# Hash attention and a max-out FFN on one core: a head's four bit tests in one, two pair hashes put together, one group hash a unit earlier

## The chip, the cores and the metric

The kernel runs on one core of a Trainium2 chip. The core has five engines that run on their own and meet through semaphores: TensorE (PE), VectorE (DVE), ScalarE (ACT), GpSimd (POOL) and SyncE (SP). The metric is the device time of one execution in microseconds. Before the change it is 268.99 us, the median of three runs (268.82 to 269.55).

## The reference, cut to what matters

```python
q_bits = (np.einsum('bhsd,dk->bhsk', q, proj) > 0)        # proj: 64 x 6
k_bits = (np.einsum('bhsd,dk->bhsk', k, proj) > 0)
mask = q_bucket[:, :, :, None] == k_bucket[:, :, None, :]  # all six bits alike
scores = np.where(mask, scale * np.matmul(q, k.T), -1e9)
attn = softmax(scores)
x = matmul(attn, v)                                        # 4 batches, 8 heads, 768 x 64
h = np.maximum(np.maximum(x @ w1, x @ w2), x @ w3)         # 3072 tokens, 512 -> 768
out = h @ w_out                                            # 768 -> 512
```

## The kernel before, in words

**How the mask is computed.** Each token gets six extra rows beside its 64 features, one for each bit, with the value +0.5 or -0.5. The product of a key's column and a query's column, 70 rows each, then holds the score and a term that is largest where all six bits agree. An exp with a bias makes everything else vanish. So scores of a head can be computed when its tile `S` has both: the features (`pair_place`, `first_place` for the first head, `place` for later ones) and the bits.

**Where the bits come from.** Batch 0 has its eight heads in four pairs (pair 0 is heads 0 and 1). A pair is loaded by `load_pair`, each head and side (side 1 is k, side 0 is q) is turned by three transposes on PE (`pair_turn`, L122), copied from PSUM to a tile `T32` by DVE or ACT (`pair_keep`, L129 or L131), and placed in `S` by POOL (`pair_place`, L136). A hash multiplies `T32` by the projection and tests the sign. There are two ways to do it. By head (`head_hash`, L169, and `head_bits`, L174): four small matmuls and four tests, each of which reads PSUM and writes six rows straight into `S`; a head has four parts, side by half of the tokens (`par`). By pair (`pair_hash`, L149 to L159): one bank for the pair, one test of 128 rows into a tile `bits` (L152), and four transfers on SP's queue (L158) that carry the bits to their rows in `S`. Pairs 0 and 1 go by head, pairs 2 and 3 by pair. Heads of the batches behind come in groups of four (`load_quad`, `turn` L200, `narrow` L205, `place` L210, `quad_hash` L219, whose four transfers at L230 are issued one unit after the hash). Groups are numbered 2 to 7; 2 and 3 are batch 1.

**What sets the order of the work.** The order is written out by hand: the instructions of an engine run in the order of the program. The main loop goes over units: a unit is 128x768 scores of one head (three matmuls of 256 columns in batch 0, two of 384 later, L296) and one exp on ACT (L304). Batch 0 has 48 units, the others 144. Two PSUM buffers hold scores, so the scores of unit n+2 wait for the exp of unit n. In iteration u the program writes the scores of unit u+1, then what `when(u, ...)` has put down for u, then one group of the FFN where there is one, then the bursts put down for u in `todo` (sums of the exps, L351, and their products with v, L373), and at last the hash of a group that `hash_at` names for u. Units 0 to 5 are head 0, 6 to 11 head 1, 12 to 23 heads 2 and 3; heads 4 to 7 begin at unit 24, two units a head for chunk 0 of queries. Units 48 to 59 are batch 1's heads 0 to 3, and from unit 60 on heads 4 to 7, group 3.

**Queues around the change.** Transfers are issued by SP (keys and queries of batch 0, placements of later groups, bits, results), by ACT (queries of pair 0) and by POOL (v, weights, queries and keys of later groups), each in the order of the program. Transfers of SP and ACT share eight completion semaphores in rotation, so an issue waits until the issue eight before it has landed.

**Before the loop.** The loads go out; 11 matmuls on a zero tile (L498) keep PE busy until the first keys are there; then head 0 is turned, hashed and tested part by part, and units 0 and 1 are written. The hash of groups uses another arrangement of the projection, `pj`, which POOL fills (L534 to L536).

Of the kernel before, what the change touches and what calls it, by code (L numbers as in the profile page):

```python
# [11 lines left out]
BF16 = mybir.dt.bfloat16  # L12
AluOp = mybir.AluOpType
# [4 lines left out]
def kernel(  # L18
# [12 lines left out]
    nc = tc.nc  # L31
# [62 lines left out]
    def give(i):  # L94
        free_banks.append(i)
# [70 lines left out]
    def head_hash(bp, pi, side, hd, pars=(0, 1)):  # L166
        for par in pars:
            j = 2 * side + par
            nc.tensor.matmul(bp[Q * j : Q * j + NBITS, 0:HALF], pj2[:, par : 2 * NBITS : 2],  # L169
                             t32[pi][:, side, hd * HALF : (hd + 1) * HALF], start=True, stop=True)  # L170

    def head_bits(bp, pi, side, hd, par):
        j = 2 * side + par
        nc.vector.tensor_scalar(out=s_tile(pi)[D : D + NBITS, 2 * side + hd, par * HALF : (par + 1) * HALF],  # L174
                                in0=bp[Q * j : Q * j + NBITS, 0:HALF], scalar1=0.0, scalar2=0.5,
                                op0=AluOp.is_gt, op1=AluOp.subtract)

    def head_rest(pi, hd):
        i, bp = bank()
        for side in (1, 0):  # L180
            head_hash(bp, pi, side, hd)
        for side, par in ((1, 0), (0, 0), (1, 1), (0, 1)):
            head_bits(bp, pi, side, hd, par)
        give(i)


    def load_quad(side, g, xs, eng):
# [284 lines left out]
    def when(u, f, *args):  # L472
        at.setdefault(u, []).append(lambda: f(*args))

    with tc.manual_schedule():
        load_pair(0, nc.sync, (1,), 0, 1)
        load_pair(0, nc.scalar, (0,), 0, 1)
        nc.sync.dma_start(pst[:], proj.rearrange("(u d) k -> d u k", d=Q))
        nc.vector.memset(warm[:], 0.0)
        make_identity(nc, iden[:])  # L480
        load_pair(0, nc.sync, (1,), 1, 2)
        load_pair(0, nc.scalar, (0,), 1, 2)
        load_pair(1, nc.sync)
        load_pair(2, nc.sync)
        load_pair(3, nc.sync)
        load_quad(1, 2, range(4), nc.sync)
        nc.vector.memset(pj2[:], 0.0)
        nc.vector.memset(ones[:], 1.0)
        for t in at_tiles:
            nc.vector.memset(blocks(t, THIRD)[:, :, THIRD : THIRD + 2], 1.0)  # L490
        for hd in range(2):
            for u in range(2):
                (nc.vector, nc.gpsimd)[hd].tensor_copy(
                    pj2[hd * D + u * Q : hd * D + (u + 1) * Q, hd : hd + 2 * NBITS - 1 : 2], pst[:, u, :])
        load_v(0)
        iw, wp = bank()
        for n in range(11):
            nc.tensor.matmul(wp[:, 0:HALF], warm[:, 0:P], warm[:], start=True, stop=True)  # L498
        give(iw)

        ik, mk = bank()
        iq, mq = bank()
        ib, bk = bank()
        jb, bq = bank()
        pair_turn(0, 1, 0, mk)
        pair_keep(0, 1, 0, mk)
        for par in range(2):
            pair_place(0, 1, par, 0, 1)
        pair_turn(0, 0, 0, mq)
        pair_keep(0, 0, 0, mq, nc.scalar)  # L510
        head_hash(bk, 0, 1, 0, (0,))
        head_bits(bk, 0, 1, 0, 0)
        first_place(0, 0, 0, mq)
        pair_place(0, 0, 1, 0, 1)
        head_hash(bq, 0, 0, 0, (0,))
        head_bits(bq, 0, 0, 0, 0)
        head_hash(mk, 0, 1, 0, (1,))
        head_bits(mk, 0, 1, 0, 1)
        give(ik)
        head_hash(mq, 0, 0, 0, (1,))  # L520
        head_bits(mq, 0, 0, 0, 1)
        give(iq)
        scores(0)
        scores(1)
        pair_turn(0, 1, 1, bk)
        pair_turn(0, 0, 1, bq)
        pair_keep(0, 1, 1, bk)
        give(ib)
        pair_keep(0, 0, 1, bq)
        give(jb)  # L530
        for side in (1, 0):
            for par in range(2):
                pair_place(0, side, par, 1, 2)
        nc.gpsimd.memset(pj[:], 0.0)  # L534
        for x in range(4):
            nc.gpsimd.tensor_copy(pj[x * Q : (x + 1) * Q, :, x : x + 4 * NBITS - 3 : 4], pst[:])  # L536

        for pi, us in ((1, ((0, 1, 0), (0, 0, 0), (3, 1, 1), (4, 0, 1))), (2, ((6, 1, 0), (7, 1, 1), (9, 0, 0), (10, 0, 1))),
                       (3, ((11, 1, 0), (13, 1, 1), (14, 0, 0), (15, 0, 1)))):
            for u, side, hd in us:  # L540
                when(u, pair_group, pi, side, hd, nc.scalar if pi == 1 and hd == 1 else None)
                if pi == 1:
                    for par in range(2):
                        when(u, pair_place, pi, side, par, hd, hd + 1)
                elif hd == 1:
                    for par in range(2):
                        when(u, pair_place, pi, side, par)
        when(2, head_rest, 0, 1)
        when(2, t32.pop, 0)
        when(5, head_rest, 1, 0)  # L550
        when(8, head_rest, 1, 1)
        when(9, t32.pop, 1)
        when(12, pair_hash, 2)
        when(13, t32.pop, 2)
        when(18, pair_hash, 3)
        when(19, t32.pop, 3)
        when(17, load_v, 1)
        for n, u in ((0, 3), (1, 12), (2, 21), (3, 31)):
            when(u, load_weights, n)
        when(13, load_quad, 0, 2, range(4), nc.gpsimd)  # L560
        for u, side, g in ((23, 1, 3), (27, 0, 3)):
            when(u, load_quad, side, g, range(4), nc.sync)
        hash_at = {}
        for g in range(2, NQUAD):
            b2, i2 = divmod(g, 2)
            need = UPB * b2 + 12 * i2
            for n, side in enumerate((1, 0)):
                name = (side, g)
                if g > 3:
                    us = [SPREAD[b2][0] + SPREAD[b2][1] * (8 * i2 + 4 * n + n2) // 4 for n2 in range(4)]  # L570
                    for x in range(4):
                        when(us[0] - 14 + x, load_quad, side, g, (x,), nc.gpsimd)
                else:
                    us = [need - {2: 26, 3: 23}[g] + 4 * n + n2 for n2 in range(4)]
                for n2, u2 in enumerate(us):
                    when(u2, turn, name, n2 // 2, n2 % 2)
                    if n2 % 2:
                        when(u2 + 1, narrow, name, n2 // 2)
                when(us[3] + 3, place, name, range(4))
            hash_at[{2: 32, 3: 48, 4: need - 12}.get(g, need - 9)] = g  # L580
            when({2: 36, 3: 46}.get(g, need - 22), load_v, g)

        ffn, credit = [], 0
        todo = {}
        last_of = {}
        for c, i in sorted(done_at, key=lambda e: done_at[e]):
            d = done_at[c, i] + LAG[c > 2]
            sums, values = burst(c, i)
            pieces = [lambda f=sums: f(0, NM), lambda f=values: f(0, 0, NM), lambda f=values: f(1, 0, NM)]
            for n, f in enumerate(pieces):  # L590
                u = {(0, 0): (16, 17, 20), (1, 0): (21, 22, 24), (2, 0): (26, 27, 29)}.get((c, i), (d, d, d))[n]
                todo.setdefault(u, []).append(f)
            last_of[c] = max(u, last_of.get(c, 0))
        ffn_at = {}
        for c in range(NCH - 1):
            ffn_at.setdefault(last_of[c] + 2, []).append(c)

        for u, (c, h, n) in enumerate(units):
            if c >= 3 and n:
                when(min(u + 2, NU - 1), add, c, h, n)  # L600

        for u in range(NU):
            if 0 < u < NU - 1:
                scores(u + 1)
            for f in at.pop(u, []):
                f()
            for c in ffn_at.get(u, []):
                ffn += ffn_groups(c)
            credit += 1 if u < UPB else 1.15
            if not ffn:  # L610
                credit = 0
            while ffn and credit >= 1:
                credit -= 1
                ffn.pop(0)()
            for f in todo.pop(u, []):
                f()
            if u in hash_at:
                when(u + 1, quad_hash(hash_at[u]))

        for f in ffn[:3]:  # L620
            f()
        ffn = ffn[3:]
        for u in sorted(todo):
            for f in todo[u]:
                f()
        ffn += ffn_groups(NCH - 1)
        for f in ffn:
            f()
# [30 lines left out]
```

## Time and profile before

| | us |
|---|---|
| median of the runs | 268.99 |
| the profiled execution's own time | 268.58 |
| its span, from the first to the last instruction | 266.6 |
| PE busy | 257.9 (97%) |
| DVE busy | 208.9 (78%) |
| ACT busy | 177.3 (67%) |
| POOL busy | 69.9 (26%) |

In the rows of the profile, `MATMUL sc<-S` are scores, `ACTIVATE AT<-sc` are exps, `ms` is one of four PSUM banks, `T` is `T32` or `T16`, and `pj` stands for both arrangements of the projection. A row of the timeline has the start in us, the length, engine, line, operation, what it writes and reads, the shape and how many instructions were merged into it; in brackets stands the idle time of the engine before it and what ended that. SP's landings have no rows of their own: they are seen in what waits for them.

### The profile page before, as it was taken

Reading aid. Unit: us, or ns where it says so; the run is one execution under the profiler, and the core shown is the slowest. Engines: PE = TensorE matmul, PEld = TensorE weight load, DVE = VectorE, ACT = ScalarE, POOL = GpSimd, SP = SyncE. Lnnn points to the kernel's source line nnn. Section 1 sums busy time; section 2 is a strip of 40 time slices with the busy share of each in tenths; the row PEclk is TensorE's granted clock in tenths of the full one; section 3 lists DMA queues with packets and bytes.
Section 4 is the critical chain, followed back from the end, with each engine's and each line's share of the span. In section 5 each row is a group of like instructions: output and inputs, shape, how many; then the busy total and the mean of one; then the engine's idle time right before and its main releaser. Section 6 shows DMA issues by size and latency. Waiting matters only on the chain.

```text
span 266.6 us, 6482 instructions
## 1 busy us (share of the span) xinstructions
PE 257.9 (97%) x2505; PEld 154.4 (58%) x2505; DVE 208.9 (78%) x493; ACT 177.3 (67%) x257; POOL 69.9 (26%) x132
## 2 busy tenths in 40 slices
PE   7899999999799999999999999999999999999995
PEld 4555557885566575555555554555555555554552
DVE  2897685987499999978998997899849785888361
ACT  3596785676758694984869578484895859581322
POOL 3588652355032535240141612011000000000000
PEclk9999999999999999999999999999999999999999
DMA  6977999969703791982054472802030003000303
GB/s 203 316 156 135 230 234 212 245 114 233 185 22 86 159 231 18 234 222 53 4 167 131 56 182 43 204 8 61 15 118 4 0 2 119 2 0 2 118 0 118
DMA packets 20717, 30.95 MB, mean 116 GB/s; under 512 B 2608, under 2 KB 15248, under 8 KB 20688
## 3 DMA queue, kind: packets, MB, share of 16 engines
q0 software_dynamic: 8128, 13.37, 26.6%
q1 hardware_dynamic: 12128, 16.66, 21.8%
q10 hardware_dynamic: 432, 0.52, 0.6%
q8 instruction: 19, 0.31, 0.5%
q14 instruction: 10, 0.08, 0.1%
HBM read 25.17 MB, written 6.29 MB: 118 GB/s over the span
## 4 chain that ended last, share of the span: by engine, by line
PE 84%; DVE 7%; ACT 5%; issue 3%; DVEq 0%; ACTq 0%
PE ms L406 31%; PE sc L296 21%; PE ms L373 11%; PE ms L450 10%; ACT AT L304 4%; PE ms L351 3%; PE ms L219 3%; DVE ht L415 2%; DVE ad L327 1%; PE ms L498 1%; PE ms L122 1%; PE ms L149 1%; DVE T L131 1%; PE ms L169 1%; DVE S L174 1%
## 5 line engine op out<-in xcount | busy, mean ns | idle before, releaser
L304 ACT ACTIVATE AT<-sc 128x768 f16<-128x768 f32 x192 | 152.3, 816 | 62.2 <-PE sc L296 60.7
L406 PE MATMUL ms<-xT,w_sb 128*128 128x384 f16 (+1 forms) x648 | 114.8, 307 | 0.1
L296 PE MATMUL sc<-S 72*128 72x384 bf16 (+1 forms) x432 | 93.6, 308 | 3.3 <-ACT AT L304 1.8
L406 PEld LDWEIGHTS <-w_sb 128*128 128x128 f16 x648 | 62.7, 97 | 35.9 <-issue 0.4
L415 DVE TENSOR_TENSOR ht<-ht,ms 128x384 f16<-128x384 f16 (+1 forms) x108 | 54.3, 504 | 24.4 <-PE ms L406 13.4
L296 PEld LDWEIGHTS <-S 72*128 72x128 bf16 (+1 forms) x432 | 39.4, 98 | 35.7 <-issue 15.5
L205 POOL TENSOR_SCALAR T<-T 128x768 bf16<-128x768 f32 x24 | 22.8, 952 | 95.4 <-issue 50.5
L450 PE MATMUL ms<-wout_sb,ht 128*128 128x512 f16 x138 | 35.5, 378 | 0.0
L373 PE MATMUL ms<-AT,vo 128*32 128x385 f16 (+3 forms) x864 | 35.2, 309 | 0.3 <-DVE ht L415 0.3
L327 DVE TENSOR_TENSOR ad<-ad,AT 128x768 f16<-128x768 f16 x48 | 26.6, 553 | 2.1 <-ACT AT L304 1.3
L373 PEld LDWEIGHTS <-vo 128*32 128x32 f16 x864 | 22.6, 96 | 9.6 <-issue 1.8
L200 DVE STREAM_TRANSPOSE T<-nat 128x384 f32<-128x384 f32 x48 | 27.0, 565 | 0.2 <-DMA nat<-in_q_dram 0.2
L327 DVE TENSOR_TENSOR ad<-AT,AT 128x768 f16<-128x768 f16 x48 | 26.2, 546 | 0.2 <-ACT AT L304 0.2
L411 ACT CAST ht<-ms 128x384 f16<-128x384 f32 x36 | 17.3, 479 | 8.1 <-PE ms L406 8.1
L380 DVE SCALAR_TENSOR_TENSOR xT<-ms,sv,rb 128x384 f16<-128x384 f32 (+1 forms) x36 | 19.8, 567 | 1.4
L450 PEld LDWEIGHTS <-ht 128*128 128x128 f16 x138 | 13.3, 97 | 13.0 <-issue 0.3
L454 ACT COPY osb<-ms 128x512 f32<-128x512 f32 x21 | 12.2, 585 | 8.2 <-PE ms L450 6.3
L330 DVE TENSOR_TENSOR ad<-ad 128x384 f16<-128x384 f16 x32 | 15.5, 484 | 1.1
L136 POOL TENSOR_SCALAR S<-T 64x384 bf16<-64x384 f32 (+1 forms) x23 | 14.2, 617 | 5.0 <-DVE T L131 3.5
L358 DVE STREAM_TRANSPOSE ys<-ms 128x384 f32<-128x384 f32 (+1 forms) x18 | 9.6, 532 | 6.2 <-PE ms L351 6.2
L194 POOL DMA_DIRECT2D nat<-in_q_dram x20 | 11.1, 560 | 0.1
L413 DVE CAST ht<-ms 128x256 f16<-128x256 f32 x18 | 7.4, 413 | 4.0 <-PE ms L406 3.9
(48 smaller groups left out, 123.0 us busy)
## 6 DMA issues: line engine op xcount, KB each, us to landing
out_dram<-osb SPq DMA_DIRECT2D x21, 256.0 KB
S<-T SPq DMA_DIRECT2D x48, 96.0 KB
nat<-in_q_dram POOLq DMA_DIRECT2D x20, 192.0 KB, 6.7
vo<-in_v_dram POOLq DMA_DIRECT2D x8, 384.0 KB, 6.2
nat<-in_k_dram POOLq DMA_DIRECT2D x16, 192.0 KB, 5.7
w_sb<-in_moe_w_dram POOLq DMA_DIRECT2D x3, 768.0 KB, 6.9
nat<-in_k_dram SPq DMA_DIRECT2D x10, 192.0 KB
nat<-in_k_dram SPq DMA_DIRECT2D x3, 384.0 KB
```

The costliest lines, as they stand in the source:

```text
L200: nc.vector.transpose(t32[name][:, u, half * HALF : (half + 1) * HALF], i_)
L205: nc.gpsimd.tensor_scalar(out=t16[name][:, u, :], in0=t32[name][:, u, :], scalar1=RS, scalar2=1.0, op0=AluOp.mult, op1=AluOp.mult)
L296: nc.tensor.matmul(views[j], s_of[kn][0 : D + bits, kx, m * P : (m + 1) * P], s_of[qn][0 : D + bits, qx, q0 : q0 + w], start=True, stop=True)
L304: nc.scalar.activation(t[:, :, 0:w], whole, ActFn.Exp, bias=-SCALE * 0.25 * bits, scale=SCALE)
L327: nc.vector.tensor_tensor(out=sum_of[c, h][:], in0=t[0], in1=t[n], op=AluOp.add)
L330: nc.vector.tensor_tensor(out=t[:, 0, :], in0=t[:, 0, :], in1=t[:, 1, :], op=AluOp.add)
L373: nc.tensor.matmul(av[Q * x : Q * (x + 1), 0:n], v_at[2 * b + i][:, x, cb * D + side : (cb + 1) * D : 2], weights_of(c, 4 * i + x, m)[:, 0 ...
L380: nc.vector.scalar_tensor_tensor(out=xt_of(c)[:, 2 * i + side, 0:w], in0=av[:, 0:w], scalar=sv_of[b, i, side][:], in1=rb[0][:, 0:w], op0=A ...
L406: nc.tensor.matmul(ps[:, 0:w], w_sb[wi][:, jc, fb * P : (fb + 1) * P], xt[:, jc, 0:w], start=(jc == 0), stop=(jc == NJC - 1))
L411: nc.scalar.copy(hts[fb][:, 0:w], ps[:, 0:w])
L415: nc.vector.tensor_tensor(out=hts[fb][:, 0:w], in0=hts[fb][:, 0:w], in1=ps[:, 0:w], op=AluOp.max)
L450: nc.tensor.matmul(ps[:, 0:DM], hts[fb][:, tb * P : (tb + 1) * P], wout_sb[:, fb, :], start=(fb == 0), stop=(fb == NFB - 1))
```

## The change: what it does

- `head_rest` makes one test of all four parts of a head, 128 rows into a tile `bits`, gives the bank back, and then copies four times six rows from `bits` into `S`.
- The projection's load moves from SP's queue, behind the first keys, to ACT's queue, ahead of the first queries. Warm-up matmuls go from 11 to 9.
- The transposes of pairs 1 to 3 are put down for other units (pair 1 from 0, 0, 3, 4 to 1, 2, 4, 5; pairs 2 and 3 from 6 to 15 to 6 to 16), the hashes by head for 3, 7 and 9 (from 2, 5 and 8), and the hash of pair 2 moves from unit 12 to unit 18, where pair 3's stands.
- POOL fills `pj` at unit 20 and not ahead of the loop.
- The first three chunks' bursts start at unit 18 and not at 16; they end one unit later.
- The hash of group 3 moves from unit 48 to 47.

```diff
@@ head_rest
         for side in (1, 0):
             head_hash(bp, pi, side, hd)
+        bits = b_pool.tile([P, HALF], BF16, tag="bits", name="bits")
+        nc.vector.tensor_scalar(out=bits[:], in0=bp[:, 0:HALF], scalar1=0.0, scalar2=0.5,
+                                op0=AluOp.is_gt, op1=AluOp.subtract)
+        give(i)
         for side, par in ((1, 0), (0, 0), (1, 1), (0, 1)):
-            head_bits(bp, pi, side, hd, par)
-        give(i)
+            j = 2 * side + par
+            nc.vector.tensor_copy(s_tile(pi)[D : D + NBITS, 2 * side + hd, par * HALF : (par + 1) * HALF],
+                                  bits[Q * j : Q * j + NBITS, :])
@@ start
         load_pair(0, nc.sync, (1,), 0, 1)
+        nc.scalar.dma_start(pst[:], proj.rearrange("(u d) k -> d u k", d=Q))
         load_pair(0, nc.scalar, (0,), 0, 1)
-        nc.sync.dma_start(pst[:], proj.rearrange("(u d) k -> d u k", d=Q))
...
-        for n in range(11):
+        for n in range(9):
             nc.tensor.matmul(wp[:, 0:HALF], warm[:, 0:P], warm[:], start=True, stop=True)
...
-        nc.gpsimd.memset(pj[:], 0.0)
-        for x in range(4):
-            nc.gpsimd.tensor_copy(pj[x * Q : (x + 1) * Q, :, x : x + 4 * NBITS - 3 : 4], pst[:])
@@ what is put down for which unit
-        for pi, us in ((1, ((0, 1, 0), (0, 0, 0), (3, 1, 1), (4, 0, 1))), (2, ((6, 1, 0), (7, 1, 1), (9, 0, 0), (10, 0, 1))),
-                       (3, ((11, 1, 0), (13, 1, 1), (14, 0, 0), (15, 0, 1)))):
+        for pi, us in ((1, ((1, 1, 0), (2, 0, 0), (4, 1, 1), (5, 0, 1))), (2, ((6, 1, 0), (8, 1, 1), (11, 0, 0), (12, 0, 1))),
+                       (3, ((13, 1, 0), (14, 1, 1), (15, 0, 0), (16, 0, 1)))):
...
-        when(2, head_rest, 0, 1)
-        when(2, t32.pop, 0)
-        when(5, head_rest, 1, 0)
-        when(8, head_rest, 1, 1)
-        when(9, t32.pop, 1)
-        when(12, pair_hash, 2)
-        when(13, t32.pop, 2)
-        when(18, pair_hash, 3)
-        when(19, t32.pop, 3)
+        when(3, head_rest, 0, 1)
+        when(3, t32.pop, 0)
+        when(7, head_rest, 1, 0)
+        when(9, head_rest, 1, 1)
+        when(10, t32.pop, 1)
+        for pi in (2, 3):
+            when(18, pair_hash, pi)
+            when(19, t32.pop, pi)
         when(17, load_v, 1)
+        when(20, nc.gpsimd.memset, pj[:], 0.0)
+        for x in range(4):
+            when(20, nc.gpsimd.tensor_copy, pj[x * Q : (x + 1) * Q, :, x : x + 4 * NBITS - 3 : 4], pst[:])
...
-            hash_at[{2: 32, 3: 48, 4: need - 12}.get(g, need - 9)] = g
+            hash_at[{2: 32, 3: 47, 4: need - 12}.get(g, need - 9)] = g
...
-                u = {(0, 0): (16, 17, 20), (1, 0): (21, 22, 24), (2, 0): (26, 27, 29)}.get((c, i), (d, d, d))[n]
+                u = {(0, 0): (18, 19, 21), (1, 0): (22, 23, 25), (2, 0): (26, 28, 30)}.get((c, i), (d, d, d))[n]
```

## The prediction, made before the changed kernel was run

> **What bounds the kernel now.** I read the page's busy shares first, then the busy time by stretch, then the timeline of each stretch in which PE is not full, then SyncE's queue.
>
> ```profile
> span 266.6 us, 6482 instructions
> PE 257.9 (97%) x2505; PEld 154.4 (58%) x2505; DVE 208.9 (78%) x493; ACT 177.3 (67%) x257; POOL 69.9 (26%) x132
> 20.00:24.00 4.00, 3.63 (x25) 1.00 0.80 160
> 69.00:73.00 4.00, 2.52 (x20) 1.00 0.63 173
> 72.00:245.00 173.00, 172.42 (x1558) 99.71 (x1558) 150.35 (x333) 121.85 (x178) 32.69 (x44) 1.00 0.33 83
> ```
>
> PE is full from 72 to 245 us (172.42 of 173.00), in an order that the program fixes. So the end follows PE: whatever PE saves before 72 us is saved at the end, and nothing that the change does after that can show. The work on PE is nearly the same in both kernels (two warm-up matmuls fewer), so the sum is one of PE's waits. There are three: the start, the stretch at 20 us, and the one before 72 us.
>
> The start, from the timeline:
>
> ```profile
> 0.74 0.89 ACTq L117 DMA_DIRECT2D nat<-in_q_dram  x2
> 1.13 3.70 PE L498 MATMUL ms<-warm 128*128 128x384 f16 x11 [1.13 <-DVE pj L487]
> 1.19 0.42 SPq L478 DMA_DIRECT2D pst<-in_proj_dram  x1
> 4.01 0.37 SPq L117 DMA_DIRECT2D nat<-in_q_dram  x1
> 4.29 0.34 DVE L493 COPY pj<-pst 32x6 f32<-32x6 f32 x2 [2.68 <-DMA pst<-in_proj_dram]
> 4.62 1.10 PE L122 MATMUL ms<-iden,nat 128*128 128x128 f32 x6
> 5.44 0.56 DVE L131 COPY T<-ms 128x384 f32<-128x384 f32 x1 [0.81 <-PE ms L122]
> 6.05 1.44 PE L169 MATMUL ms<-T,pj 128*6 128x384 f32 x8 [0.32 <-DVE T L131]
> 6.90 2.31 DVE L174 TENSOR_SCALAR S<-ms 6x384 bf16<-6x384 f32 x4 [0.90 <-PE ms L169]
> 8.08 0.49 PE L296 MATMUL sc<-S 70*128 70x256 bf16 x3 [0.60 <-DVE S L174]
> 8.61 1.51 ACT L304 ACTIVATE AT<-sc 128x768 f16<-128x768 f32 x2 [1.98 <-PE sc L296]
> ```
>
> Eleven warm-ups issue from 1.13 to 4.62, 0.32 apart ((4.62 - 1.13) / 11). The loads issued at 0.74 have landed by 4.01, when SyncE, which waited for that completion, goes on; so the first transposes stand behind warm-ups. Then one chain: transpose, copy, hash, four tests one after the other, scores.
>
> The middle:
>
> ```profile
> 14.59 2.96 ACT L304 ACTIVATE AT<-sc 128x768 f16<-128x768 f32 x4
> 16.61 0.83 PE L169 MATMUL ms<-T,pj 128*6 128x384 f32 x8
> 17.38 0.50 PE L296 MATMUL sc<-S 70*128 70x256 bf16 x3
> 18.04 0.49 PE L296 MATMUL sc<-S 70*128 70x256 bf16 x3
> 18.07 2.26 DVE L174 TENSOR_SCALAR S<-ms 6x384 bf16<-6x384 f32 x4
> 20.39 1.89 PE L149 MATMUL ms<-T,pj 128*32 128x384 f32 x8 [0.37 <-DVE S L174]
> 22.20 0.50 PE L296 MATMUL sc<-S 70*128 70x256 bf16 x3
> 25.50 0.50 PE L296 MATMUL sc<-S 70*128 70x256 bf16 x3
> 26.72 0.50 PE L296 MATMUL sc<-S 70*128 70x256 bf16 x3
> 27.15 0.85 PE L149 MATMUL ms<-T,pj 128*32 128x384 f32 x8
> 28.10 0.56 DVE L152 TENSOR_SCALAR bits<-ms 128x384 bf16<-128x384 f32 x1 [0.54 <-PE ms L149]
> 39.87 0.84 PE L351 MATMUL ms<-AT,ones 128*32 128x256 f16 x24
> ```
>
> These rows give the prices of a chain. A head's hash takes 0.77 on PE (16.61 to 17.38), a unit of scores with one group of transposes 0.66 (17.38 to 18.04, so 0.33 each), a unit with a burst of 24 matmuls 1.22 (25.50 to 26.72). An exp starts 0.53 after its scores (8.08, 8.61); two take 1.51 and four 2.96, so they follow 0.72 apart and one takes 0.8. With two score buffers, unit n+2 waits for exp n, about 0.85 after that exp began. Pair 2's hash stalls: DVE is busy with four tests (18.07, 2.26), the copies that feed the hash queue behind them, and L149 holds PE from 20.39 to 22.20, where the same hash of pair 3 needs 0.8 (its row at 27.15 says 0.85, the last result's way out included): 1.0 us lost, and the 0.4 that the row names in front of it.
>
> **The change, part by part.** Start: two warm-ups fewer free PE 0.64 earlier, at 3.98; k has landed by 4.01, q, now issued 0.45 later behind proj, by the time that proj lands today (before 4.29), and its transposes come third to sixth, after 4.6. Proj lands earlier, off the path. So the chain moves by 0.63: first scores at 7.45. The gain is between 0 (loads late) and 0.64; I take 0.6. Nothing else waits on ACT's queue: the third issue there is 0.4 of an engine that idles until 5.
>
> Tests: four of 0.55 become one of 0.56 (row L152 above, the same shape) and four copies of 6x384 from SBUF. No such copy is in the trace; its bounds:
>
> ```profile
> L174 DVE TENSOR_SCALAR S<-ms 6x384 bf16<-6x384 f32 x16 | 8.9, 554 | 2.0 <-PE ms L169 1.7
> L493 DVE COPY pj<-pst 32x6 f32<-32x6 f32 x2 | 0.3, 160 | 2.7 <-DMA pst<-in_proj_dram 2.7
> L136 POOL TENSOR_SCALAR S<-T 64x384 bf16<-64x384 f32 x15 | 7.6, 506 | 3.7 <-DVE T L131 2.8
> L158 SPq DMA_DIRECT2D S<-bits x8: 722/722/960, 22.9 to 31.0; - x8
> ```
>
> At least 0.16 (L493), at most 0.55 (as from PSUM). I take 0.2, nearer to the copy in SBUF, since it is a copy there too. A head then costs DVE 1.36, not 2.26; but the first two bits, which the next scores need, come after 0.56 + 0.4 = 0.96, against 1.11 today: nearly no gain on the path.
>
> Order up to unit 18, chained by the prices above: unit 0 at 7.45; 1 at 8.15; 2 at 9.1 behind two groups; 3 at 9.8; 4 at 10.5; head 1's hash from 10.8; unit 5 at 11.6; unit 6 needs its bits: 10.83 + 0.90 (hash to DVE, as 6.05 to 6.90 and a little) + 0.96 + 0.2 = 12.9. Then exp sets the pace: exp 6 at 13.4, two copies of ACT's between, exp 7 at 14.6, exp 8 to 10 at 15.3, 16.0, 16.7; head hash before unit 11, exp 11 at 17.8; then 0.72 a unit: unit 14 at 19.4, unit 19 at 22.9. The stall of pair 2's hash is gone, since its copies are long done; in its place PE waits a little for each exp, since the bursts that filled those gaps start two units later. Hash of pair 2 begins at H = 23.3.
>
> From H, PE alone: two hashes 1.6, sums 0.8 (a burst of 24, as the row at 39.87), unit 20 and a burst 1.22, unit 21 0.33, units 22 and 23 with a burst each 2.44: unit 24, the first to use head 4, could go at H + 6.4 = 29.7. Its bits: DVE done at H + 0.95 + 0.56; SyncE issues k's then q's (0.72 to 0.96 each), so q's goes out at H + 2.45. What landing costs is the main unknown. Rows that bound it:
>
> ```profile
> 30.22 1.49 SPq L158 DMA_DIRECT2D S<-bits  x2
> 36.58 0.31 SPq L194 DMA_DIRECT2D nat<-in_q_dram  x1
> ```
>
> SyncE rotates eight completion semaphores; the load at 36.58 waits for the issue eight back, the second of these two (about 30.98). So 9 KB took 5.6 us, while POOL's loads filled the DMA engines. At H the same loads are ahead (one of the weights and four of queries, in POOL's queue just before pair 3's last placements in both programs), so I take 5.3, a little less than this last one, as q's goes out earlier in the train: landing at H + 7.75 = 31.0, unit 24 at 31.1, a new stall of 1.4. Bounds: 3.3 (the first loads, 0.74 to 4.01), no stall; 8.3 (shown below for group 3), a stall of 4.4. From 31.1: units 24 and 25 1.56, unit 26 at 32.8 (its bits at H + 9.4), 26 to 28 with bursts 2.4, 28 and 29 with a burst 1.56, unit 31 at 37.3 behind its exp, a burst, unit 33 at 38.9, chunk 0's second sums at 39.3, against 39.87: 0.6 gained to that place, with all work before it alike.
>
> Moved without cost: pj's memset and copies go from 12.5 to behind the v load on POOL; they are needed at unit 32's hash, near 41, and POOL idles there. The first weights' load moves ahead of two placements and shares the engines with pair 3's loads, which are used after 19. SyncE's next loads, behind eight bit transfers, go out near 31.2, where they go now (31.8).
>
> Group 3's hash back at 47:
>
> ```profile
> 57.96 0.84 PE L351 MATMUL ms<-AT,ones 128*32 128x256 f16 x24
> 59.95 1.46 PE L219 MATMUL ms<-T,pj 128*32 128x384 f32 x16
> 62.08 2.94 SPq L230 DMA_DIRECT2D S<-bits  x4
> 62.17 2.18 POOL L194 DMA_DIRECT2D nat<-in_q_dram  x4
> 69.87 0.60 PE L406 MATMUL ms<-xT,w_sb 128*128 128x256 f16 x4
> 71.95 0.48 PE L296 MATMUL sc<-S 72*128 72x384 bf16 x2 [1.48 <-ACT AT L304]
> ```
>
> The wait before 71.95 is put down to ACT, which had long been done; it is group 3's bits. The third issue, q's, at about 63.6 is used at 71.95: 8.3 us. Unit 60 could go at 69.87 + 0.44 = 70.31, so 1.64 is lost. Today the hash stands behind the burst of sums and values (57.96 to 59.95). In the change it stands ahead of it, 2 us and a unit earlier, so bits go out as soon as SyncE has placed the queries, near 59; and POOL's later key and query loads, which stand behind buffers that this burst frees, come 1.3 later. Even with 8.3 us they land by 69: the stall goes, 1.64. What is late next is the exp that frees unit 60's buffer; it runs in step with PE there, so I put it at nothing.
>
> Sum: -0.6 and -1.64 = -2.2 on the profiled execution's 268.58 (span 266.6 and 2.0 around it). It lies 0.4 under the median of the runs, 268.99, so I predict 266.8. 0.3% (0.8 us) is what a measurement can tell.
>
> **Rivals.** (a) Bits land in 3.3 us: unit 24 does not wait, 1.4 more is gained, of which group 2's bits, which are in a chain on SyncE, may take back 0.2 at unit 48: 265.6. For it: they are 9 KB. Against: 5.6 in the trace with the same traffic.
> The Trainium skill's page "DMA: Bandwidth & Descriptors", section "Queues, rings and completion order", has each engine go round its queues packet by packet, which would let a small transfer pass a big load; by it (a) would hold. The 5.6 us speak against it.
>
> (b) Slower: bits land in 8.3 us at unit 24 too. Then unit 24 goes at 34.2 and second sums at 42.3, 2.4 later than now; with 1.64 back the kernel ends 0.8 late: 269.8. It decides from 7.5 us on. For it: the eight transfers go out in one train behind four query loads, as group 3's do now. Against: pair 3's, also behind four loads.
>
> (c) Copies wait for POOL, which places queries at the same time: with one placement (0.51) before each, a copy costs 0.7, unit 6 goes 1.0 later and unit 12 0.1: 267.9. For it: POOL has back-to-back work there. Against: the DVE copies at 4.29 took 0.16 while POOL copied too.
> The Trainium skill's page "SBUF — State Buffer", section "SBUF: two separate sides", says that DVE in a two-port mode and GpSimd exclude each other for a whole instruction; by it the copies would wait so. No run here shows a wide one.
>
> (d) The move to 47 does nothing, since the bits end with POOL's loads whenever they start: only -0.6, 268.4.
>
> **Chances.** Forecast 0.40 (own range 266.0 to 267.6), (a) 0.13, (b) 0.22, (c) 0.11, (d) 0.10, something not seen, slower, 0.04. Faster: 0.39 + 0.13 + 0.08 of (c) = 0.60; same: 0.01 + 0.03 of (b) + 0.03 of (c) + 0.08 of (d) = 0.15; slower 0.25. The range, 265.2 to 270.0, holds (a) to (b).
>
> **What would show it.** First scores near 7.5; L149 once, 1.6 long, near 23; four copies of about 0.2; a gap in PE of about 1.4 before a score unit near 31 with ACT idle; second sums near 39.3; no gap at 70. Wrong if PE waits longer than 3 us near 30, or the gap at 70 stays.

## The result, and the profile after

The changed kernel is slower. Its median over six runs is 273.25 us (272.07 to 274.96), against 269.12 us (268.29 to 270.55) for the kernel before in the same session: a ratio of 1.0153, with a 95% interval of 1.0108 to 1.0198. The profiled execution took 272.87 us, with a span of 270.9. The prediction was 266.8 with a range of 265.2 to 270.0; the measured time lies above the range.

Lines of the changed kernel are five higher than before from the scores on: scores L301, exps L309, sums L356, products with v L378, loads of a group L199. The test of a head is L183, its copies are L188.

The busy shares of the page hardly move, but its clock row now has a dip in the sixth slice (a slice is 6.8 us):

```profile
span 270.9 us, 6481 instructions
PE 258.9 (96%) x2503; PEld 155.0 (57%) x2503; DVE 209.5 (77%) x496; ACT 177.4 (65%) x257; POOL 70.0 (26%) x132
PEclk9999959999999999999999999999999999999999
```

The timeline of PE, from the joint hash to the second sums of chunk 0 (which stood at 39.87 before):

```profile
24.90 1.50 PE L149 MATMUL ms<-T,pj 128*32 128x384 f32 x16
30.18 0.84 PE L356 MATMUL ms<-AT,ones 128*32 128x256 f16 x24
35.32 0.80 PE L301 MATMUL sc<-S 70*128 70x256 bf16 x3 [4.30 <-DMA S<-bits]
36.05 1.47 PE L378 MATMUL ms<-AT,vo 128*32 128x256 f16 x24
42.21 0.84 PE L378 MATMUL ms<-AT,vo 128*32 128x256 f16 x24
45.57 0.84 PE L356 MATMUL ms<-AT,ones 128*32 128x256 f16 x24
```

Two losses stand there. The burst at 30.18 occupies PE for 0.78 (as from 26.21 to 26.99 in the same timeline), so unit 24 could have gone at 30.96; it went at 35.32, 4.36 us late, and the row names the transfers of bits. Then bursts of 24 matmuls take 1.47, where the same burst takes 0.84 at 42.21. The busy time by stretch shows why (columns: stretch and its length, busy time of PE, PEld, DVE, ACT and POOL, granted clock, DMA share, GB/s):

```profile
35.30:40.50 5.20, 5.18 (x60) 2.75 (x60) 1.56 (x4) 2.32 (x3) 0.83 (x1) 0.52 1.10 220
40.50:45.50 5.00, 4.88 (x93) 3.15 (x90) 4.36 (x11) 3.99 (x6) 1.53 (x2) 1.00 1.10 242
```

Behind the wait PE runs at about half of its clock for 5.2 us, and at full clock again after that. Together the second sums come 5.70 later than before (45.57 against 39.87). The gap ahead of unit 60 is gone: units 59 and 60 follow each other 0.76 apart, with one group of the FFN between them.

```profile
75.45 0.49 PE L301 MATMUL sc<-S 72*128 72x384 bf16 x2
76.21 0.49 PE L301 MATMUL sc<-S 72*128 72x384 bf16 x2
```

Unit 60 went at 71.95 before, so it comes 4.26 later: 1.44 of the 5.70 is won back, where the prediction counted 1.64. So the account by the profile closes: 268.58 + 4.26 = 272.84, against 272.87 of the profiled execution.

The queues show what the bits waited behind. SP's first two issues of bits, then POOL's queue:

```profile
26.40 1.75 SPq L158 DMA_DIRECT2D S<-bits  x2
```

```profile
24.27 0.75 POOL L251 DMA_DIRECT2D w_sb<-in_moe_w_dram  x1
25.02 2.23 POOL L199 DMA_DIRECT2D nat<-in_q_dram  x4
```

Both transfers that unit 24 needs were out by 28.15; it went 7.2 us after that. POOL had sent off a load of weights (768 KB) and four loads of queries (192 KB each) ahead of them and beside them.

### The profile page after: what moved, and what is told of

It is laid out like the page before. It is cut to its first block, busy times and chain, and to the rows that moved or that the text cites. A ratio compares the mean times of both kernels' runs of the same rounds, so it can differ in the third digit from the quotient of the medians.

```text
span 270.9 us, 6481 instructions
## 1 busy us (share of the span) xinstructions
PE 258.9 (96%) x2503; PEld 155.0 (57%) x2503; DVE 209.5 (77%) x496; ACT 177.4 (65%) x257; POOL 70.0 (26%) x132
## 3 DMA queue, kind: packets, MB, share of 16 engines
q0 software_dynamic: 8128, 13.37, 26.8%
## 4 chain that ended last, share of the span: by engine, by line
PE 85%; DVE 5%; ACT 3%; DMA 3%; issue 1%; POOL 1%; SPq 0%; DVEq 0%; ACTq 0%
PE ms L411 32%; PE sc L301 21%; PE ms L378 11%; PE ms L455 11%; ACT AT L309 3%; PE ms L224 3%; DMA S<-bits 3%; PE ms L356 2%; DVE ad L332 1%; DVE ht L420 1%; PE ms L503 1%; POOL S L136 1%; PE ms L122 1%; PE ms L169 1%; DVE S L174 1%
## 5 line engine op out<-in xcount | busy, mean ns | idle before, releaser
L309 ACT ACTIVATE AT<-sc 128x768 f16<-128x768 f32 x192 | 152.4, 816 | 67.0 <-PE sc L301 63.4
L301 PE MATMUL sc<-S 72*128 72x384 bf16 (+1 forms) x432 | 94.3, 311 | 7.1 <-DMA S<-bits 4.3
L301 PEld LDWEIGHTS <-S 72*128 72x128 bf16 (+1 forms) x432 | 39.8, 98 | 38.8 <-issue 13.3
L378 PE MATMUL ms<-AT,vo 128*32 128x385 f16 (+3 forms) x864 | 36.5, 316 | 0.3 <-DVE ht L420 0.3
L378 PEld LDWEIGHTS <-vo 128*32 128x32 f16 x864 | 23.1, 99 | 10.3 <-issue 2.2
L363 DVE STREAM_TRANSPOSE ys<-ms 128x384 f32<-128x384 f32 (+1 forms) x18 | 9.6, 534 | 4.7 <-PE ms L356 4.6
L199 POOL DMA_DIRECT2D nat<-in_q_dram x20 | 11.0, 560 | 0.1
```

The costliest lines, as they stand in the source:

```text
L301: nc.tensor.matmul(views[j], s_of[kn][0 : D + bits, kx, m * P : (m + 1) * P], s_of[qn][0 : D + bits, qx, q0 : q0 + w], start=True, stop=True)
L309: nc.scalar.activation(t[:, :, 0:w], whole, ActFn.Exp, bias=-SCALE * 0.25 * bits, scale=SCALE)
L378: nc.tensor.matmul(av[Q * x : Q * (x + 1), 0:n], v_at[2 * b + i][:, x, cb * D + side : (cb + 1) * D : 2], weights_of(c, 4 * i + x, m)[:, 0 ...
```

## The experiments

The theory after this reading: joining pair 2's hash to pair 3's puts the bits of head 4 behind POOL's loads, and this wait, with the half clock behind it, is the loss. Rivals: the new work of DVE (the copies), the later order of the transposes, or the train of eight transfers on SP itself.

### Pair 2's hash taken back to an earlier unit (14)

```diff
-        for pi in (2, 3):
-            when(18, pair_hash, pi)
-            when(19, t32.pop, pi)
+        when(14, pair_hash, 2)
+        when(15, t32.pop, 2)
+        when(18, pair_hash, 3)
+        when(19, t32.pop, 3)
```

> The changed kernel with pair 2's hash at unit 14 (pair 3's stays at 18). Theory A (the loss is the wait of unit 24 for pair 2's bits, 4.5 us, and the half clock behind it, about 2 us): no gap before unit 24 and the clock stays full, so about 6.5 less than the changed kernel's 273.25, 266.8, below the kernel before by about 2. Rival B (the loss is made earlier, by the order up to unit 18 and by slow copies): unit 24 late anyway, 271 or more.

Measured: 268.49 us, a ratio of 1.0006 (0.9984 to 1.0029). All of the slowdown goes, but nothing is gained either, though the hash at 47 is still in it. The timeline of PE:

```profile
30.90 0.50 PE L301 MATMUL sc<-S 70*128 70x256 bf16 x3
35.73 0.81 PE L301 MATMUL sc<-S 70*128 70x256 bf16 x6 [0.63 <-DMA S<-bits]
41.82 1.52 PE L378 MATMUL ms<-AT,vo 128*32 128x257 f16 x48 [1.14 <-DMA vo<-in_v_dram]
```

Unit 24 goes at 30.90 without a wait. What eats the rest are two more landings: bits of pair 3 ahead of unit 28 (35.73), and v ahead of the products at 41.82, a load that stands in POOL's queue behind the later placements.

### Zero matmuls into the wait

```diff
+        def fill():
+            iw, wp = bank()
+            for n in range(26):
+                nc.tensor.matmul(wp[:, 0:HALF], warm[:, 0:P], warm[:], start=True, stop=True)
+            give(iw)
```

It is called once, ahead of unit 24's scores; all else is the changed kernel.

> The changed kernel with 26 matmuls of 384 columns on the zero tile (4.2 us of PE at full clock, no use made of them) in front of unit 24, where PE sits idle for 4.5 us. Theory A says that the idle time itself costs more, by the clock at 0.52 in the 5 us behind it: the stretch from unit 24 to unit 27 took 4.9 us and takes 2.8 at full clock, so about 2.1 less: 271.1. If the low clock costs nothing, or comes from something else than the idle PE: 273.2, and the granted clock stays near 0.5 there.

Measured: 270.36 us, a ratio of 1.0082 (1.0064 to 1.0099). The busy time by stretch:

```profile
35.30:40.50 5.20, 5.20 (x111) 3.51 (x112) 3.40 (x9) 3.75 (x5) 0.83 (x1) 1.00 1.13 231
```

The clock stays at 1.00, through the filled wait too, and PE issues 111 matmuls in the stretch in which it issued 60. Unit 24 goes at 35.34, as in the changed kernel, and the second sums at 43.39, 2.18 earlier. So the low clock is PE's answer to standing idle, and is worth 2.2 us in the profile, 1.9 by the two ratios (0.0071 of 269).

### POOL's loads behind the bits

```diff
-        for n, u in ((0, 3), (1, 12), (2, 21), (3, 31)):
+        for n, u in ((0, 3), (1, 22), (2, 25), (3, 31)):
             when(u, load_weights, n)
-        when(13, load_quad, 0, 2, range(4), nc.gpsimd)
+        when(22, load_quad, 0, 2, range(4), nc.gpsimd)
```

> The changed kernel with POOL's second load of weights and its four loads of queries put down for unit 22 and not 12 and 13, so that the DMA engines are empty when pair 2's bits go out. Only unit 24 is looked at, since the queries come too late for their own use. Theory A, with POOL's loads as what the bits wait for: bits land in about 3 us and the gap before unit 24 is under 1 us. Rival C (the bits are slow by themselves, eight transfers in a train on one queue): the gap stays at 3 us or more.

One execution: 274.44 us. The train of eight is the same, with its first two issues at the same distance from the hash, but the loads come behind it; SP's queue and PE's timeline:

```profile
26.04 1.75 SPq L158 DMA_DIRECT2D S<-bits  x2
```

```profile
30.59 0.50 PE L301 MATMUL sc<-S 70*128 70x256 bf16 x3
44.00 1.48 PE L378 MATMUL ms<-AT,vo 128*32 128x257 f16 x24 [2.79 <-DVE ys L363]
```

Unit 24 does not wait: at most 2.8 us after the issue (27.79) both transfers were there, against 7.2 behind the loads. In the same stretch, 26.40 to 30.60, the changed kernel and this one have, in the columns above:

```profile
26.40:30.60 4.20, 4.20 (x100) 2.81 (x96) 3.47 (x10) 2.63 (x4) 3.88 (x6) 1.00 1.03 213
```

```profile
26.40:30.60 4.20, 4.20 (x97) 2.60 (x86) 3.36 (x10) 3.00 (x4) 3.93 (x10) 1.00 0.36 40
```

The DMA engines are full (1.03) in the one and at 0.36 in the other. So the loads ahead set the landing, not SP's train. The packets of each queue say it too (queue, kind, packets, MB, share of 16 engines). From 26.40 to 30.50, with five of the eight transfers of bits issued, the changed kernel moved packets of q0 alone, which is POOL's queue (its 13.37 MB in all are the sum of POOL's loads); this kernel moved 36 packets of SP's queue, q1, in about as long a stretch (26.04 to 30.10):

```profile
q0 software_dynamic: 283, 0.86, 103.6%
```

```profile
q1 hardware_dynamic: 36, 0.02, 2.0%
```

So the bits were not slow on their way: they didn't start. The whole is still slow: PE stops ahead of 44.00 for a small transpose on DVE (L363), which stands behind DVE's transposes of the late queries, and the clock falls there again (0.54 from 44 to 50).

```profile
43.04 0.58 DVE L205 STREAM_TRANSPOSE T<-nat 128x384 f32<-128x384 f32 x1 [8.02 <-DMA nat<-in_q_dram]
```

### The group hash at 47 alone, and with the start

```diff
-            hash_at[{2: 32, 3: 48, 4: need - 12}.get(g, need - 9)] = g
+            hash_at[{2: 32, 3: 47, 4: need - 12}.get(g, need - 9)] = g
```

> The kernel before with nothing but group 3's hash at 47. If the gap before unit 60 was the late hash: it goes, 1.6 less, 267.4. If bits end with POOL's loads whenever they start: 269.

Measured: 266.81 us, a ratio of 0.9949 (0.9932 to 0.9965): 1.4 us less (0.9 to 1.8). The bits go out at 59.21, and unit 60 goes in step, at 70.41 and not at 71.95:

```profile
70.41 0.49 PE L296 MATMUL sc<-S 72*128 72x384 bf16 x2
```

The second kernel has the start as well: the projection on ACT's queue ahead of the queries, and nine warm-ups.

```diff
+        nc.scalar.dma_start(pst[:], proj.rearrange("(u d) k -> d u k", d=Q))
         load_pair(0, nc.scalar, (0,), 0, 1)
-        nc.sync.dma_start(pst[:], proj.rearrange("(u d) k -> d u k", d=Q))
...
-        for n in range(11):
+        for n in range(9):
```

> The kernel before with two parts of the change: group 3's hash at 47, and the start (proj on ACT's queue ahead of the queries, nine warm-ups for eleven). The hash at 47 alone gave 266.8. Theory: the queries land late behind proj, first scores near 7.9 (the changed kernel had 7.87, the kernel before 8.08): 266.6. Rival, the prediction's: first scores at 7.45, 266.2. Rival: the 0.2 to 0.6 is lost again at the exps and tests before unit 20: 266.8.

Measured: 266.59 us, a ratio of 0.9954 (0.9928 to 0.9980), not to be told from the hash alone. In its timeline the first transposes start 0.64 earlier, and nothing of that is left at the first scores, which were at 8.08 before:

```profile
3.98 1.49 PE L122 MATMUL ms<-iden,nat 128*128 128x128 f32 x6
5.48 1.79 PE L169 MATMUL ms<-T,pj 128*6 128x384 f32 x8
6.84 2.31 DVE L174 TENSOR_SCALAR S<-ms 6x384 bf16<-6x384 f32 x4 [1.41 <-PE ms L169]
8.02 0.49 PE L296 MATMUL sc<-S 70*128 70x256 bf16 x3 [0.76 <-DVE S L174]
```

The first hash starts 0.57 earlier than before (6.05), the first test only 0.06 (6.90): the test now begins 1.36 behind the hash's start, 0.85 before. That is PE's pace in this one execution. The kernel with pair 2's hash at 14, the first experiment, has the same start, and its first hash begins at 5.48 too; here are the first record of that hash in this kernel, the same in that one, and that one's first scores:

```profile
5.48 0.81 PE L169 MATMUL ms<-T,pj 128*6 128x384 f32 x1
```

```profile
5.48 0.49 PE L169 MATMUL ms<-T,pj 128*6 128x384 f32 x1
7.52 0.49 PE L301 MATMUL sc<-S 70*128 70x256 bf16 x3 [0.41 <-DVE S L174]
```

PE starts at half its pace in every execution (the last section has the rows) and comes to the full one sooner in some than in others. Over all profiled executions, the first scores are at 7.51 to 8.02 in the seven with this start (middle one 7.75), and at 7.82 to 8.46 in the seven with the old one (middle one 8.15). So the start gains about 0.4, which the times of this pair of kernels can't show.

### The joint hash alone

```diff
-        when(12, pair_hash, 2)
-        when(13, t32.pop, 2)
-        when(18, pair_hash, 3)
-        when(19, t32.pop, 3)
+        for pi in (2, 3):
+            when(18, pair_hash, pi)
+            when(19, t32.pop, pi)
```

> The kernel before with one thing changed: pair 2 is hashed at unit 18 with pair 3, not at unit 12. Theory: this alone makes the loss. The 1.4 of the stall at 20.4 us are saved, but the hashes come near 25.5, the bits of head 4 go out behind POOL's loads and land near 35 or 36, as in the changed kernel; unit 24, which could go near 31, waits 3.5 to 4.5, and the granted clock falls for 5 us behind it (2 to 3 us more): 268.5 - 1.4 + 3.5 + 2.9 = 273.5, or 270.6 to 271.5 if the clock stays full. Rival, as the prediction sized it: bits land 5.3 to 5.6 after their issue, a wait of 1 to 1.5: 268.3. Rival: it needs the other parts too (loads moved ahead, groups later), and the time stays at 268.5 or below.

Measured: 272.04 and 272.56 us, a ratio of 1.0158 (1.0132 to 1.0184), 4.2 us more. This one edit is as slow as the whole change. PE's timeline has the same wait:

```profile
34.07 1.44 PE L296 MATMUL sc<-S 70*128 70x256 bf16 x6 [3.26 <-DMA S<-bits]
35.44 1.47 PE L373 MATMUL ms<-AT,vo 128*32 128x256 f16 x24
```

Two more executions took 277.83 and 277.90 us and are not in the ratio. The profile is of the one at 277.90 (span 275.9), so its rows give the place of the wait and the half rate behind it, not their price.

### The one test alone, and the copies by themselves

The edit is `head_rest` alone, as in the change, on the kernel before.

> The kernel before with one thing changed: a head's four tests are one test and four copies. Theory: a copy that meets a placement on POOL ends only about 0.11 behind it (0.25 alone, up to 0.88 then), so a head saves DVE little, and unit 6's bits come no earlier: within 0.4 of 268.5, with copies of a mean near 0.4. Rival, the prediction's: 0.2 each, a head saves 0.9, and the stall of pair 2's hash (1.4) shrinks by about that: 267.6. Rival: unit 6 and unit 12 go later by the waits, 0.5 to 1.0: 269.2.

Measured: 269.71 us, a ratio of 1.0069 (1.0037 to 1.0102): 1.9 us slower. DVE and PE in its timeline, at the last head:

```profile
18.56 0.55 DVE L183 TENSOR_SCALAR bits<-ms 128x384 bf16<-128x384 f32 x1
19.14 2.41 DVE L188 COPY S<-bits 6x384 bf16<-6x384 bf16 x4
21.58 1.49 DVE L131 COPY T<-ms 128x384 f32<-128x384 f32 x3
22.19 1.30 PE L149 MATMUL ms<-T,pj 128*32 128x384 f32 x4 [1.26 <-DVE T L131]
```

Test and copies take 2.99 where four tests took 2.26, so the copies of T that feed pair 2's hash start at 21.58 and not at 20.36. The stall that the prediction wanted to shrink grows, and chunk 0's second sums come at 41.09, 1.22 later than before.

What a copy waits for is seen one by one. Busy time by stretch in the changed kernel, line L188 alone (stretch and length, DVE busy, clock, DMA share, GB/s), and POOL in the same place:

```profile
19.45:19.98 0.53, 0.52 (x1) 1.00 1.06 212
20.00:20.89 0.89, 0.88 (x1) 1.00 0.95 183
20.91:21.17 0.26, 0.25 (x1) 1.00 0.50 95
```

```profile
19.94 0.83 POOL L136 TENSOR_SCALAR S<-T 64x768 bf16<-64x768 f32 x1
```

The second copy starts just after a placement (19.94 to 20.77) and ends 0.11 behind it; the third, with POOL idle, takes 0.25. The Trainium skill's page "SBUF — State Buffer", section "SBUF: two separate sides", says that DVE, in a fast mode that takes both port pairs, and GpSimd hold the shared pair one at a time for a whole instruction. These rows agree: 0.25 alone, up to 0.88 behind a placement.

Next, the same kernel with the test's result in f32, so that the copies convert:

```diff
-        bits = b_pool.tile([P, HALF], BF16, tag="bits", name="bits")
+        bits = o_pool.tile([P, DM], FP32, tag="osb", name="bits")
...
```

> The kernel of e8 (the kernel before with one test and four copies for a head; 269.7, copies of 0.455 in the mean) with the one test's result kept in f32, so that the copies read f32 and write bf16. Theory: the bf16 copies are fast alone (0.25) and wait for POOL's placements because of the fast form; the f32 ones would be slower alone, but would not wait: all copies equal, 0.40 to 0.50 whether POOL is busy or not, none above 0.55, and pair 2's hash ends 0.3 to 0.5 earlier than in e8: 269.3. Rival: any DVE copy between SBUF tiles waits for POOL: copies from 0.25 to 0.9 as in e8, 269.7 or more. Rival: the spread comes from something else than POOL, and f32 copies are 0.25 to 0.9 without a tie to POOL's ends.

Measured: 272.26 us, a ratio of 1.0111 (1.0040 to 1.0181). The theory's guess was wrong: these copies wait too. In the same view, line L188:

```profile
15.46:15.82 0.36, 0.35 (x1) 1.00 1.16 213
20.06:20.96 0.90, 0.89 (x1) 1.00 0.98 133
```

0.35 alone, 0.89 behind a placement, 0.515 in the mean. The mean of the bf16 copies was 0.455, so twelve copies explain 0.7 of the 2.5 us between these two kernels; PE also waits 1.65 ahead of the second half of pair 2's hash, and the clock stands at 0.50 from 22.71 to 26.12. So for both types a copy between SBUF tiles waits for POOL, while the tests, which read PSUM, stay at 0.55 beside the same placements.

### Four tests, and pair 1's transposes back

Two kernels look for the rest of the loss on the kernel with pair 2's hash at 14. The first takes back the four tests of `head_rest`:

```diff
-        bits = b_pool.tile([P, HALF], BF16, tag="bits", name="bits")
...
         for side, par in ((1, 0), (0, 0), (1, 1), (0, 1)):
+            head_bits(bp, pi, side, hd, par)
+        give(i)
```

> The kernel of e1 (pair 2's hash at unit 14, everything else as changed) with the four tests from PSUM back in place of one test and four copies. In the changed kernel the copies took 0.25 where POOL was quiet and up to 0.88 where POOL was placing, 0.42 in the mean, so a head costs DVE 0.56 + 4 x 0.42 = 2.24 against 4 x 0.55 = 2.2: theory, the copies bring and cost about nothing, and unit 6, which needs two of them (0.25 + 0.48, against 0.55 with one test fewer ahead), goes at most 0.25 earlier: 268.2 to 268.5. The 1.6 us that e1 loses beside the hash at 47 is then the order of the groups and bursts. Rival: the copies are that 1.6: 267.0, with no wait before unit 6 and none near 20 us. Rival: exp sets the pace there, no change at all, 268.5.

Measured: 268.06 us, a ratio of 0.9990 (0.9970 to 1.0011). Little comes back, since in this order a landing ends the stretch again, here the bits of head 5, in pair 2's train, ahead of unit 26 (the next expectation calls them pair 3's):

```profile
34.08 0.49 PE L296 MATMUL sc<-S 70*128 70x256 bf16 x3 [1.28 <-DMA S<-bits]
```

The second also puts pair 1's transposes back to their units:

```diff
-        for pi, us in ((1, ((1, 1, 0), (2, 0, 0), (4, 1, 1), (5, 0, 1))),
+        for pi, us in ((1, ((0, 1, 0), (0, 0, 0), (3, 1, 1), (4, 0, 1))),
```

> The kernel with pair 2's hash at 14 and four tests (e5, 0.999 of the kernel before), with the groups of transposes of pair 1 back at units 0, 0, 3, 4 from 1, 2, 4, 5. Theory: the groups' later units are what is left of the loss: unit 6 waited there until 13.32 for POOL's placement of head 2's keys and queries, and goes near 12.6 when the groups are back; 0.6 to 0.8 less, ratio 0.996 to 0.997, unless the later wait for pair 3's bits (1.28 before 34.08) takes some of it back. Rival: that wait takes all of it back, since the bits land when POOL's loads let them: ratio 0.999. Rival: exp paces PE between 12 and 25 us, so nothing changes after unit 12.

Measured: 270.02 us, a ratio of 1.0068 (1.0016 to 1.0120). The theory fell: in this order, later transposes were a gain, not a loss. Unit 6 goes at 14.35 with them early and at 13.32 with them late; PE then waits 1.13 for the same bits, and this time the clock falls too. Timeline and busy time by stretch:

```profile
35.02 0.49 PE L296 MATMUL sc<-S 70*128 70x256 bf16 x3 [1.13 <-DMA S<-bits]
```

```profile
33.30:36.71 3.41, 2.28 (x45) 1.26 (x41) 2.56 (x6) 1.91 (x3) 2.65 (x5) 1.00 1.08 208
36.71:40.13 3.42, 3.42 (x46) 2.00 (x50) 2.54 (x8) 2.01 (x3) 0.09 (x1) 0.50 1.21 246
```

### What beats both kernels

The kernel before with the group hash at 47 and pair 2's hash one or two units later, at 13 or 14, ahead of POOL's query loads:

```diff
-        when(12, pair_hash, 2)
-        when(13, t32.pop, 2)
+        when(13, pair_hash, 2)
+        when(14, t32.pop, 2)
```

> The kernel before with group 3's hash at 47 (which alone gave 266.8, span 264.8) and pair 2's hash one unit later, at 13 (its T given up at 14). Theory: at unit 12 the hash stands 1.4 us on PE because the copies that feed it queue behind four tests; one unit later 0.66 of that is other work, so 0.5 to 0.7 are gained, and head 4's bits go out about as early as before, so that unit 24 does not wait: 266.2. Rival: the stall is only handed to the exps, which set the pace there: 266.8. Rival: the bits come later behind POOL's loads and unit 24 waits 1 to 4: 268 to 270.

> As the kernel with pair 2's hash at 13, but at 14 (T given up at 15). Theory: two units of other work, 1.3 of the 1.4, stand ahead of it, and the bits still go out before POOL's query loads: 265.6 to 266.2, unit 24 near 30 without a wait. Rival: the bits go out 1.3 later and fall behind POOL's loads, so unit 24 waits by 1 or more: 267 to 268. Rival: exp sets the pace, 266.8.

Measured: 266.62 us at 13, a ratio of 0.9928 (0.9906 to 0.9949), and 266.82 us at 14, 0.9930 (0.9906 to 0.9954). Both beat the two kernels compared; beside the group hash alone (0.9949) the intervals overlap, so a gain of the later hash isn't shown. At 13 the hash takes 1.21 and not 1.89, and unit 24 goes at 30.96 with no wait:

```profile
20.83 1.21 PE L149 MATMUL ms<-T,pj 128*32 128x384 f32 x8
30.96 0.83 PE L296 MATMUL sc<-S 70*128 70x256 bf16 x6
```

## Why the prediction was wrong

The step that failed is the landing of the bits: "so I take 5.3", with a new stall of 1.4. The hash is the 24.90 row, and the issue of q's bits began 2.5 behind it, as the prediction had it; but the landing took 7.9 from there (27.4 to 35.3). The stall is 4.36. The 5.6 us on which the size rested was right as read and wrong as a guide: those bits, too, had POOL's loads ahead, but how much lies ahead decides, as the two kernels with the loads before and behind the train show (7.2 and at most 2.8). Rival (b), with its bound of 8.3 and its point of decision at 7.5, was the true case; the chance given to it was 0.22.

A second term was not in the sum at all: the clock. The page's clock row is full in the kernel before, and a longer idle time of PE was priced at its own length. It cost 2.2 us more. With it, rival (b)'s 269.8 becomes 272.0; most of the rest of the distance to 272.87 goes with the late hash, below.

Point by point:

- Start, -0.6: too large. First scores at 7.87 in the changed kernel, not at 7.45, and about 0.4 earlier than with the old start over all profiled executions. Two things were off. PE's pace at the start, which differs by execution, was not in the sum. And the landing of q was put before 4.29; PE waited for it until 4.76:

```profile
4.76 0.50 PEld L122 LDWEIGHTS ms<-iden,nat 128*128 128x128 f32 x3 [0.34 <-DMA nat<-in_q_dram]
```

- Copies, 0.2 each: wrong by a factor of two, 0.416 in the mean:

```profile
L188 DVE COPY S<-bits 6x384 bf16<-6x384 bf16 x12 | 5.0, 416 | 0.4
```

  Rival (c) had the mechanism, and the argument against it (copies of 32x6 that took 0.16 while POOL copied too) was too small a row to carry it. In the kernel before, that edit alone costs 1.9 us.
- The order up to the hash: unit 6 at 13.70 against 12.9, unit 14 at 20.99 against 19.4, H at 24.90 against 23.3. Ahead of unit 14 stand the two copies of 0.52 and 0.88 shown above, 1.4 where 0.4 was assumed. At unit 23 PE was 0.94 ahead of the kernel before (29.75 against 30.69), but 0.78 of that is a burst of sums that stood ahead of unit 23 before (at 29.91) and stands behind it now (30.18). Up to the second sums the new order saved 0.84 (4.36 + 2.18 - 5.70), where the prediction had 2.0 (a gain of 0.6 beside a stall of 1.4).
- "Wrong if PE waits longer than 3 us near 30": this is what came.
- The moves "without cost" leave out v. Its load stands behind the later placements, and with pair 2's hash at 14, where the wait is gone, it stops PE for 1.14.
- Group 3's hash at 47, -1.64: right. The gap went; with that edit alone the bits went out at 59.21 ("near 59"), and it is worth 1.4 us (0.9 to 1.8). Rival (d) is out.
- Rival (a), 3.3 us: out for this order, and true (at most 2.8) where POOL's loads come behind. The rule of the Trainium skill's page "DMA: Bandwidth & Descriptors", section "Queues, rings and completion order", that an engine serves its queues in turn by packets, would have let these 9 KB pass the loads; the 7.2 us speak against leaning on it, and so do the 4.1 us in which POOL's packets alone moved.

What stays open: how much of the rest belongs to the later bursts and to the later transposes of pairs 2 and 3, which no run took back by themselves, and what besides idle time brings the clock down.

## What to carry to other kernels

A small transfer on the path should be issued ahead of large loads from another queue, and its landing priced by the bytes that are under way at that moment, not by its own size. A wait on PE is to be priced with the matmuls behind it at half rate: here this came behind waits from 1.13 us on, though not behind each of them. A copy between SBUF tiles on DVE is not cheap beside a POOL that works on SBUF: take its time from a row with POOL busy. One profiled execution is a poor measure of a gain of a few tenths at the start.

## What the runs showed of the hardware that was not expected

The granted clock fell behind PE's waits, in stretches of 3.41 us at 0.50, and not at all when zero matmuls filled the same time. In the changed kernel it was low for two such stretches, from 33.42 to 40.25:

```profile
30.01:33.42 3.41, 1.01 (x27) 0.55 (x24) 2.79 (x8) 1.05 (x2) 3.19 (x8) 1.00 1.04 245
33.42:36.84 3.42, 1.52 (x19) 0.89 (x23) 0.00 (x0) 0.62 (x1) 0.82 (x1) 0.50 1.33 174
```

The Trainium skill's page "TensorE: Matmul & The Clock Gate", section "What's actually happening", has the clock halved after an idle window of about 3.4 us, with windows that run freely. The trace agrees with the length of the window and not with an idle one: PE was busy 1.01 of the 3.41 us ahead of the fall, which came 2.4 into the wait of 4.30. With pair 1's transposes back it was busy 2.28 of the 3.41 ahead of the fall (the rows are with that experiment), and with the f32 copies 1.77. But with the bf16 copies on the kernel before, the clock stayed full behind a stretch with 2.15 busy (19.97 to 23.38, a wait of 1.26), and no run here shows what decides between these. The six runs of the changed kernel spread with it: one stretch at half the clock is 0.006 of a span of 271 us, and the mean clock was 0.994 in the fastest run (272.07 us), 0.987 in three (272.50 to 273.64) and 0.981 in the two slowest (274.10 and 274.96).

PE also starts slowly, and the clock column doesn't show it: it says 1.00 from 1.2 to 3.0 us. There the warm-up matmuls follow each other 0.32 apart, as worked out in the prediction. The same matmuls in the filled wait, 26 of them from 31.11 to the scores at 35.34, follow each other 0.16 apart:

```profile
31.11 4.40 PE L563 MATMUL ms<-warm 128*128 128x384 f16 x26
```

A copy of six rows of 384 between SBUF tiles takes 0.25 us (bf16) or 0.35 (f32 to bf16) alone and up to 0.89 when a placement on POOL is ahead of it; it ends 0.11 behind the placement.
